# A three-stage layer on one core: the prologue and first pass in another order, six half-tile normalisings on the activation engine, and the last routing in one run

## The chip, the cores and the metric

The kernel runs on one core of one Trainium2 chip. TensorE (PE) multiplies matrices, VectorE (DVE) and ScalarE (ACT) work on elements, GpSimd (POOL) issues gathers and scatters with indices, SyncE (SP) issues the plain loads and stores. The metric is the device time in microseconds (us) of one launch; lower is better. The kernel before takes 1042.08 us (median of 3 runs, 1041.61 to 1042.24).

## The reference

```python
scores = scale * q @ k.T              # 4 x 8 heads, 576 positions, 64 wide
scores = where(0 <= i - j < 64, scores, -1e9)
x = softmax(scores) @ v               # window attention -> x: 2304 x 512
g = sigmoid(x @ w_gate) * (x @ w_val) # 512 -> 1536
x = g @ w_out                         # 1536 -> 512
noisy = x @ w_gate2 + log1p(exp(x @ w_noise)) * noise   # 8 experts
top2, weights = the two largest of noisy, softmax over the two
out[t] = sum over its two experts of weight * (relu(x[t] @ w1[e]) @ w2[e])   # 512 -> 1024 -> 512
```

Everything is float32. The dense layer's three weights are handed over as the 64-bit integers of doubles, which the kernel turns into float32 itself.

## The kernel before

Every large product is three matmuls, on a high and a low half of each operand (`mm3`, L55 to L58), so each operand must first be split: the high half by ACT, the low half by DVE.

The tokens stand in 18 tiles of 128 and 6 blocks of 3 tiles. The dense layer goes block by block; inside a block it goes over 12 slices `f` of 128 hidden columns. For a slice PE makes the gate and the value (12 matmuls of 384 columns each), ACT takes the tanh, DVE multiplies, ACT and DVE split the product, and PE adds it to the output (9 matmuls of 512 columns). The first block has more to do: its three tiles of attention must be there first, and during it the weights of each slice are converted, by three ACT steps (L187, L192, L222) and four DVE steps (L197, L202, L208, L231) on 128 x 1536 elements. Slice 0 is converted in thirds of 512.

The order of this prologue and first pass is written out by hand as a string of words, `FIRST`; each engine runs its part of it in that order. A letter is a step and a number the slice or attention tile; `a` and `b` are halves of four heads. The steps that the text speaks of:

- weights: `m` (ACT, L187), `r` (ACT, L192), `s` (DVE, L197), `o` (DVE, L202), `a` (DVE, L208), `h` (ACT, L216 or L222), `l` (DVE, L229 or L231). `r` and `a` share one buffer, `rnd`.
- attention of a tile: `S` scores (PE, L244), `M` mask and maximum (DVE, L258), `E` exponential (ACT, L269), `N` the sums' reciprocals (DVE, L274, L275) and the normalising of four heads (DVE, L280), `P` transposes (PE, L286), `C` their copy (ACT, L292), `O` times v (PE, L307), `H` and `X` the split of the result (ACT L316, DVE L321).
- the slice: `g` and `V` gate and value (PE), `t` tanh (ACT, L337), `u` multiply (DVE, L342), `q` and `w` the split (ACT L349, DVE L353), `y` output (PE, label acc).

`g0` and `V0` are cut: columns 0 to 255 (`a`) need tiles 0 and 1, the rest (`b`) needs tile 2, that is the third L321. All loads go out on SP's queue; before, they hang on certain words (`S0`, `O0`, `O2`) and on a list ahead of the string.

After the dense layer's last block come the last block's routing (`route_L1`, `La`, `Lb`, `Lc`, `P`, `Q`, on DVE with two small matmuls in `P`), the scatter of its rows into the experts' slot tables (POOL, L522), and the gather of the fifth tile of expert 0. PE meanwhile works on the first four tiles of expert 0: per slice `h_mm` (12 matmuls of 512 columns), `h_ev` (relu on ACT, low half on DVE, L711 and L712) and `y_mm`; `split_e` makes the halves of the next slice's weights (L654 to L657). Then the experts follow one after the other, eight slices each. At the end of an expert `y_out` scales the five tiles and scatters each by an adding DMA (POOL, L745).

Of the kernel before, what the change touches and what calls it, by code (L numbers as in the profile page):

```python
# [11 lines left out]
F32R = mybir.dt.float32r  # L12
# [3 lines left out]
AF = mybir.ActivationFunctionType  # L16
# [3 lines left out]
P = 128  # L20
# [15 lines left out]
CAP = CT * P  # L36
# [9 lines left out]
def build(nc, tc, a, out):  # L46
# [27 lines left out]
    qk0 = pa.tile([P, 4, P + 192], F32, name="qk", bufs=1)  # L74
# [46 lines left out]
    noise = const.tile([P, TT, 8], F32)  # L121
# [5 lines left out]
    with c1:  # L127
# [106 lines left out]
        Sp, Pt, PT, Ox = {}, {}, {}, {}  # L234
# [29 lines left out]
        def attn_E(t, cs):  # L264
            sm, st = Pt[t]
            for c in cs:
                if c not in En.setdefault(t, set()):
                    En[t].add(c)
                    nc.scalar.activation(sm[:, c], sm[:, c], AF.Exp, bias=st[:, 0, c:c + 1], scale=-1.0,  # L269
                                         accum_out=st[:, 1, c:c + 1])  # L270

        def attn_R(t, cs=slice(0, 8)):
            st = Pt[t][1]
            nc.vector.tensor_scalar(st[:, 1, cs], st[:, 1, cs], 1e-9, None, op0=OP.add)  # L274
            nc.vector.reciprocal(st[:, 2, cs], st[:, 1, cs])  # L275

        def attn_N(t, g):
            sm, st = Pt[t]
            c = slice(g * 4, g * 4 + 4)
            nc.vector.tensor_tensor(sm[:, c], sm[:, c], st[:, 2, c, None].to_broadcast([P, 4, P]), op=OP.mult)  # L280
# [97 lines left out]
        R = {}  # L378
# [152 lines left out]
        def fill_slots():  # L531
# [10 lines left out]

        FIRST = """
            r00 m00 s00 S0 o00 a00 h00 S1 M0b l00 E0b M0a M1b E0a M1a N0b r01 m02 N0a P0b m01 r02 s02 P0a o02
            E1a a02 S2 s01 o01 h02 a01 C0a E1b N1a M2b h01 N1b E2b l01 l02 C0b N2b m1 P1b M2a O0 r1 s1 o1 E2a
            S3 a1 C1b H0 P2b m2 X0 N2a P1a h1 s2 o2 C1a r2 O1 l1 C2b a2 m3 M3b H1 h2 X1 s3 P2a r3 l2 g0a
            C2a E3b o3 O2 m4 a3 V0a H2 s4 h3 X2 o4 g0b r4 V0b l3 t0 g1 u0 m5 a4 V1 q0 s5 r5 w0 M3a y0 t1 h4 u1
            o5 E3a g2 l4 q1 V2 w1 m6 N3a a5 t2 y1 s6 r6 g3 o6 h5 u2 S4 a6 q2 V3 w2 h6 l5 y2 t3 r7 l6 g4 m7 u3  # L550
            N3b q3 P3a s7 m8 V4 w3 o7 C3a t4 P3b u4 y3 C3b M4a q4 w4 E4a a7 y4 s8 h7 O3 o8 r8 g5 l7 H3 V5 t5
            X3 m9 a8 g6 u5 h8 s9 M4b V6 q5 r9 w5 l8 t6 y5 E4b u6 N4a q6 V7 N4b m10 w6 o9 g7 a9 P4a t7 y6 C4a u7
            h9 s10 o10 q7 g8 r10 l9 V8 a10 m11 P4b S5 w7 C4b s11 r11 y7 o11 h10 M5a O4 t8 M5b E5a g9 u8 l10 H4
            V9 q8 E5b w8 X4 N5a y8 t9 u9 a11 q9 S6 w9 P5a h11 N5b y9 C5a l11 P5b g10 C5b M6a O5 t10 V10 H5 X5
            g11 u10 q10 w10 V11 t11 y10 u11 q11 w11
        """
        SB = (("S0", "S1"), ("gate", "val"), ("acc0", "acc1"))

        def first(word):
            k, n = word[0], word[1:]  # L560
            if k in "mrsoahl":
                fn = {"m": cv_m, "r": cv_r, "s": cv_s, "o": cv_o, "a": cv_a, "h": cv_h, "l": cv_l}[k]
                if len(n) == 2 and n[0] == "0":
                    fn(0, slice(int(n[1]), int(n[1]) + 1))
                else:
                    fn(int(n))
                return
            if k in "gV":
                cols = {"a": slice(0, 2 * P), "b": slice(2 * P, BW)}.get(n[-1], slice(0, BW))
                glu_in(0, int(n.rstrip("ab")), "gV".index(k), cols)  # L570
                return
            g = "ab".find(n[-1])
            t = int(n.rstrip("ab"))
            heads = range(4 * g, 4 * g + 4)
            if k == "S":
                attn_S(t, SB[t] if t < len(SB) else ("S0", "S1"))
                if t == 0:
                    load_qk(3)
                    load_raw(2)
                elif t > 2:  # L580
                    load_qk(t + 1)
            elif k == "M":
                attn_M(t, heads)
            elif k == "E":
                attn_E(t, heads)
            elif k == "N":
                attn_R(t, slice(4 * g, 4 * g + 4))
                attn_N(t, g)
            elif k == "P":
                attn_PT(t, g, ("OP", "acc2")[g] if t < 3 else "OP")  # L590
            elif k == "C":
                attn_PC(t, g)
            elif k == "O":
                attn_O(t)
                if t == 0:
                    load_vv(3)
                    for f in range(3, 8):
                        load_raw(f)
                elif t > 2:
                    load_vv(t + 1)  # L600
                elif t == 2:
                    nc.sync.dma_start(noise, a["moe2_noise"].rearrange("(t p) e -> p t e", p=P))
                    fill_slots()
                    for f in range(8, NF1):
                        load_raw(f)
            elif k == "H":
                attn_XH(t)
            elif k == "X":
                attn_X(t)
            elif k == "y":  # L610
                glu_out(0, t)
            else:
                {"t": lambda f: glu_tanh(), "u": glu_mul, "q": glu_high, "w": glu_low}[k](t)

        nc.sync.dma_start(qk0[:, 0:1], a["qk"][0, :, 0:1])
        load_raw(0, (0,))
        nc.sync.dma_start(qk0[:, 1:4], a["qk"][0, :, 1:4])
        load_qk(1)
        load_vv(0)
        load_raw(0, (1, 2))  # L620
        load_vv(1)
        load_qk(2)
        load_vv(2)
        load_raw(1)
        for word in FIRST.split():
            first(word)


        NCH = NF2 // 2
        YB = ("gate", "val", "acc0", "acc1", "acc2")  # L630
        ep, rawc, sp = {}, {}, {}
# [73 lines left out]
                hp[e, f].append(o)  # L705

        def h_ev(e, f, cols=ALL):
            hh = ep[0].tile([P, CAP], F32R, tag="hh", name="hh", bufs=2)
            hl = ep[0].tile([P, CAP], F32R, tag="hl", name="hl", bufs=2)
            for o, c in zip(hp.pop((e, f)), cols):  # L710
                nc.scalar.activation(hh[:, c], o, AF.Relu)  # L711
                nc.vector.scalar_tensor_tensor(hl[:, c], o, 0.0, hh[:, c].bitcast(F32),  # L712
                                               op0=OP.max, op1=OP.subtract)
            hS[e, f] = (hh, hl)
# [134 lines left out]
        b = NB - 1  # L849
        pre = range(EARLY // P)  # L850
# [14 lines left out]
        route_L1(b)  # L865
        h_mm(0, 1, PRE)
        route_La(b)
        h_ev(0, 1, PRE)
        y_mm(0, 0, pre)
        split_e(2)  # L870
        h_mm(0, 2, PRE)
        route_Lb(b)
        h_ev(0, 2, PRE)
        route_Lc(b)
        y_mm(0, 1, pre)
        split_e(3)
# [34 lines left out]
    for n in range(NA, NE * NF2):  # L911
        e, f = divmod(n, NF2)
        h_mm(e, f)
        h_ev(e, f)
        split_e(n + 2)
        if n < NE * NF2 - 1:
            y_mm(*y_prev)
        if f == 0:
            for j in range(CT):
                y_out(e - 1, j)  # L920
        if 0 < e < NE - 1 and f >= NF2 - CT:
            xg_T(e + 1, f - NF2 + CT)
        if f == 0 and 0 < e < NE - 1:
            table(e + 1, slice(0, CT))
            gather(e + 1, slice(0, CT))
        y_prev = (e, f)
    for j in range(CT):
        for i in range(len(y_parts(NE - 1, j))):
            for f in (NF2 - 2, NF2 - 1):
                y_mm(NE - 1, f, (j,), (i,))  # L930
        y_out(NE - 1, j)
    ce.close()
# [82 lines left out]
```

## Time and profile before

| what | value |
|---|---|
| median of 3 runs | 1042.08 us |
| the profiled execution: time, span | 1041.44 us, 1039.6 us |
| PE busy | 1002.0 us (96%) |
| DVE, ACT, POOL busy | 577.6, 385.5, 153.2 us |
| granted clock of PE over the span | 0.981 |
| moved by DMA | 126.78 MB, mean 122 GB/s |

The profiled execution's time is 1.9 us over its span: the program's start and end lie around it. PE's busy share says little by itself, since its matmuls overlap; the idle time before a group, the chain that ended last and the start times in the timeline tell where it waits.

### The profile page before, as it was taken

How to read it: one execution, taken by the hardware profiler on the slowest of the kernel's cores; microseconds unless marked ns; L12 is line 12 of the kernel's file. 1: busy time of each engine (PE TensorE's matmuls, PEld its weight loads, DVE VectorE, ACT ScalarE, POOL GpSimd, SP SyncE). 2: the span in 40 equal slices, each digit the busy share in tenths (PEclk: the TensorE clock that was granted, in tenths of full speed). 3: DMA queues.
4: the chain of work that ended last, by engine and by line, in shares of the span. 5: the costliest groups of instructions: out<-in, count | busy, mean ns of one | idle time of the engine just before them, and what ended most of it. 6: DMA issues, size and time to landing. Idle time of an engine off the chain costs nothing.

```text
span 1039.6 us, 16682 instructions
## 1 busy us (share of the span) xinstructions
PE 1002.0 (96%) x6460; PEld 914.2 (88%) x6460; DVE 577.6 (56%) x1608; ACT 385.5 (37%) x874; POOL 153.2 (15%) x210
## 2 busy tenths in 40 slices
PE   4699999999999999999999999999999999999995
PEld 3699899999999999999998799999989999999994
DVE  7999657667767767774326434344334343434431
ACT  7887533233333333321114233333333333333321
POOL 0000000002000200302030505050311305050303
PEclk7799999999999999999999999999999999999998
DMA  8970322233333223336224417262443627172503
GB/s 344 351 280 21 133 88 83 94 117 93 102 117 107 93 101 118 83 103 219 76 70 164 128 58 192 71 161 103 93 133 92 171 82 182 44 181 82 92 1 54
DMA packets 56568, 126.78 MB, mean 122 GB/s; under 512 B 13968, under 2 KB 14112, under 8 KB 56480
## 3 DMA queue, kind: packets, MB, share of 16 engines
q1 hardware_dynamic: 46304, 104.56, 29.5%
q0 software_dynamic: 10176, 21.07, 10.0%
q8 instruction: 53, 0.87, 0.3%
q14 instruction: 35, 0.29, 0.1%
HBM read 101.11 MB, written 24.49 MB: 121 GB/s over the span
## 4 chain that ended last, share of the span: by engine, by line
PE 87%; issue 4%; DMA 3%; ACT 2%; POOL 1%; DVE 1%; SPq 0%; POOLq 0%; DVEq 0%; ACTq 0%
PE gv L56 10%; PE gv L57 10%; PE gv L58 10%; PE hp L58 6%; PE hp L57 6%; PE hp L56 6%; PE yacc L56 6%; PE yacc L57 6%; PE yacc L58 6%; PE acc L56 5%; PE acc L58 5%; PE acc L57 5%; DMA raw<-in_moe_w 2%; PE Op L307 2%; PE xgp L687 2%
## 5 line engine op out<-in xcount | busy, mean ns | idle before, releaser
L56 PE MATMUL gv<-xT,W 128*128 128x384 f32 (+2 forms) x584 | 201.2, 344 | 0.0
L57 PE MATMUL gv<-xT,W 128*128 128x384 f32 (+2 forms) x584 | 196.6, 337 | 0.8 <-DVE xT L321 0.8
L58 PE MATMUL gv<-xT,W 128*128 128x384 f32 (+2 forms) x584 | 196.6, 337 | 0.0
L712 DVE SCALAR_TENSOR_TENSOR hl<-hp,hh 128x320 fp32r<-128x320 f32 (+2 forms) x128 | 62.9, 491 | 199.8 <-ACT hh L711 197.7
L56 PE MATMUL hp<-xgT,h 128*128 128x320 f32 (+2 forms) x512 | 162.3, 317 | 0.0
L58 PE MATMUL hp<-xgT,l 128*128 128x320 f32 (+2 forms) x512 | 159.5, 312 | 0.0
L57 PE MATMUL hp<-xgT,h 128*128 128x320 f32 (+2 forms) x512 | 159.4, 311 | 0.0
L711 ACT ACTIVATE hh<-hp 128x320 fp32r<-128x320 f32 (+2 forms) x128 | 56.0, 438 | 219.7 <-PE hp L58 219.7
L420 DVE CUSTOM_DVE_ANT_0 dump<-x,wb 128x512 bf16<-128x512 f32 x192 | 132.1, 688 | 3.1
L56 PE MATMUL yacc<-h,hh 128*128 128x512 f32 (+1 forms) x328 | 127.5, 389 | 0.0
L57 PE MATMUL yacc<-l,hh 128*128 128x512 f32 (+1 forms) x328 | 127.1, 387 | 0.0
L58 PE MATMUL yacc<-h,hl 128*128 128x512 f32 (+1 forms) x328 | 126.8, 386 | 0.0
L522 POOL DMA_INDIRECT slots<-rec,sli x36 | 39.0, 1084 | 524.3 <-DMA wb<-in_wgn 249.4
L745 POOL DMA_INDIRECT out<-yo,tb x40 | 66.3, 1659 | 328.2 <-ACT yo L741 319.7
L56 PEld LDWEIGHTS gv<-xT,W 128*128 128x128 f32 x584 | 110.3, 189 | 4.1 <-issue 2.1
L57 PEld LDWEIGHTS gv<-xT,W 128*128 128x128 f32 x584 | 110.4, 189 | 2.6 <-DVE xT L321 0.9
L58 PEld LDWEIGHTS gv<-xT,W 128*128 128x128 f32 x584 | 110.3, 189 | 0.0
L342 DVE SCALAR_TENSOR_TENSOR th<-th,gv 128x384 f32<-128x384 f32 x72 | 39.8, 553 | 119.8 <-PE gv L58 100.1
L56 PEld LDWEIGHTS hp<-xgT,h 128*128 128x128 f32 x512 | 96.4, 188 | 2.2 <-DVE hl L712 0.4
L57 PEld LDWEIGHTS hp<-xgT,h 128*128 128x128 f32 x512 | 96.4, 188 | 1.9
L58 PEld LDWEIGHTS hp<-xgT,l 128*128 128x128 f32 x512 | 96.2, 188 | 1.3 <-DVE l L655 0.2
L56 PE MATMUL acc<-W,gH 128*128 128x512 f32 x216 | 86.4, 400 | 0.0
(137 smaller groups left out, 1526.2 us busy)
## 6 DMA issues: line engine op xcount, KB each, us to landing
raw<-in_moe_w SPq DMA_DIRECT2D x36, 512.0 KB
wb<-in_wgn SPq DMA_DIRECT2D x32, 512.0 KB
r<-in_w SPq DMA_DIRECT2D x32, 512.0 KB
r<-in_moe_w SPq DMA_DIRECT2D x32, 512.0 KB
qk<-in_qk SPq DMA_DIRECT2D x15, 640.0 KB
v<-in_v SPq DMA_DIRECT2D x32, 256.0 KB
out<-zero SPq DMA_DIRECT2D x26, 256.0 KB
xd<-x SPq DMA_DIRECT2D x6, 768.0 KB
```

The costliest lines, as they stand in the source:

```text
L56: nc.tensor.matmul(o, lh, rh, start=start, stop=False)
L57: nc.tensor.matmul(o, lh, rl, start=False, stop=False)
L58: nc.tensor.matmul(o, ll, rh, start=False, stop=stop)
L307: nc.tensor.matmul(o[h * 64:(h + 1) * 64, r * P + i * 64:r * P + (i + 1) * 64], v[:, i, r * P + h * 64:r * P + (h + 1) * 64], pt[:, c:c + 64],
L342: nc.vector.scalar_tensor_tensor(g, g, 1.0, gv.pop(1)[:, :BW], op0=OP.add, op1=OP.mult)
L420: nc.vector.tensor_tensor_reduce(out=dump, in0=x2[b][:, j], in1=WB[8 * b + c // 2][:, c % 2], op0=OP.mult, op1=OP.add, scale=1.0, scalar=0 ...
L522: st = nc.gpsimd.indirect_dma_start(out=slots, out_offset=bass.IndirectOffsetOnAxis(ap=sli[:, k, j:j + 1], axis=0), in_=rec[:, j, k, :], i ...
L687: nc.tensor.transpose(p[:, c], xg[:, c], ident)
L711: nc.scalar.activation(hh[:, c], o, AF.Relu)
L712: nc.vector.scalar_tensor_tensor(hl[:, c], o, 0.0, hh[:, c].bitcast(F32), op0=OP.max, op1=OP.subtract)
L745: st = nc.gpsimd.indirect_dma_start(out=out, out_offset=bass.IndirectOffsetOnAxis(ap=tb[:, j, 0:1].bitcast(I32), axis=0), in_=yo, in_offse ...
```

## The change

- `FIRST` is another string. Loads are words of it now (`K`: `Kr` raw weights, `Kq`, `Kz` q and k, `Kv` v, `Kf` the filler of the slot tables), so their order on SP's queue stands in the string; the noise comes last.
- `N` no longer takes the reciprocals along; they are the word `R`. `n` normalises four heads on ACT, one instruction for each; `n3b n3a n4a n4b n5b n5a` replace six `N`.
- `hh` and `hl` have three buffers instead of two.
- In the last routing `Lb`, `Lc` follow `La`, and `P`, `Q` follow the next `h_mm`, ahead of the `h_ev` that stood before them.
- The last expert's sixth slice is no longer added to the output between the last two `h_mm`, but with the last two slices, tile by tile.

```diff
         FIRST = """
-            r00 m00 s00 S0 o00 a00 h00 S1 M0b l00 E0b M0a M1b E0a M1a N0b r01 m02 N0a P0b m01 r02 s02 P0a o02
...
+            Kr00 Kq0 Kz0 Kr01 Kq1 Kv0 Kr02 m00 r00 Kv1 s00 o00 Kq2 a00 S0 Kv2 h00 m01 l00 Kr1 r01 Kf0 M0a Kq3
...
+            elif k == "R":
+                attn_R(t, slice(4 * g, 4 * g + 4))
             elif k == "N":
-                attn_R(t, slice(4 * g, 4 * g + 4))
                 attn_N(t, g)
+            elif k == "n":
+                sm, st = Pt[t]
+                for c in heads:
+                    nc.scalar.activation(sm[:, c], sm[:, c], AF.Copy, scale=st[:, 2, c:c + 1])
...
-        nc.sync.dma_start(qk0[:, 0:1], a["qk"][0, :, 0:1])
-        load_raw(0, (0,))
...
         for word in FIRST.split():
             first(word)
+        load_qk(7)
+        load_vv(6)
+        nc.sync.dma_start(noise, a["moe2_noise"].rearrange("(t p) e -> p t e", p=P))
...
-            hh = ep[0].tile([P, CAP], F32R, tag="hh", name="hh", bufs=2)
-            hl = ep[0].tile([P, CAP], F32R, tag="hl", name="hl", bufs=2)
+            hh = ep[0].tile([P, CAP], F32R, tag="hh", name="hh", bufs=3)
+            hl = ep[0].tile([P, CAP], F32R, tag="hl", name="hl", bufs=3)
...
         route_La(b)
+        route_Lb(b)
+        y_mm(0, 0, pre)
+        route_Lc(b)
         h_ev(0, 1, PRE)
-        y_mm(0, 0, pre)
         split_e(2)
         h_mm(0, 2, PRE)
-        route_Lb(b)
+        route_P(b)
+        route_Q(b)
         h_ev(0, 2, PRE)
-        route_Lc(b)
         y_mm(0, 1, pre)
         split_e(3)
-        route_P(b)
         h_mm(0, 3, PRE)
-        route_Q(b)
...
-        if n < NE * NF2 - 1:
+        if n < NE * NF2 - 2:
             y_mm(*y_prev)
...
-            for f in (NF2 - 2, NF2 - 1):
+            for f in range(NF2 - 3, NF2):
                 y_mm(NE - 1, f, (j,), (i,))
```

DVE in the prologue, before: from the second tile's `X` (L321) to the third's. `m0` and `m1` hold the even and odd slices in turn; `raw_332` is slice 3, `raw_336` slice 4.

```order
L321 TENSOR_TENSOR xT_312<-Op_404,xT_312 128x4x128
L197 TENSOR_SCALAR m1_122<-m1_122 128x1536
L231 TENSOR_TENSOR W_433<-m0_121,W_433 128x3x512
L202 SCALAR_TENSOR_TENSOR m1_122<-raw_332,m1_122 128x1536
L536 TENSOR_SCALAR early_120<-early_120 128x144
L537 TENSOR_SCALAR early_120<-early_120 128x144
L208 ISA m1_122<-m1_122,rnd_125 128x3072
L197 TENSOR_SCALAR m0_121<-m0_121 128x1536
L321 TENSOR_TENSOR xT_312<-Op_464,xT_312 128x4x128
```

DVE at the same place, changed: from the third tile's `X` on (`raw_337` is slice 3).

```order
L321 TENSOR_TENSOR xT_288<-Op_459,xT_288 128x4x128
L208 ISA m0_121<-m0_121,rnd_125 128x3072
L197 TENSOR_SCALAR m1_122<-m1_122 128x1536
L202 SCALAR_TENSOR_TENSOR m1_122<-raw_337,m1_122 128x1536
L342 SCALAR_TENSOR_TENSOR th_542<-th_542,gv_437 128x384
L231 TENSOR_TENSOR W_419<-m1_122,W_419 128x3x512
```

The last step of slice 2 (L208) and all steps of slice 3 stand behind the third `X` now; before, slice 3 and the first step of slice 4 stood ahead of it.

ACT in the last routing, before, from the routing's first exponential (`u`) on; `hh` is the relu of a slice, `h` the high halves of the next slice's weights, `ee` the routing's second exponential.

```order
L435 ACTIVATE u<-u 128x24
L711 ACTIVATE hh<-hp 128x512
L654 ACTIVATE h_5705<-r_5574 128x512
L656 ACTIVATE h_5707<-r_5575 128x512
L465 ACTIVATE ee<-ee 128x6
```

ACT at the same place, changed.

```order
L435 ACTIVATE u<-u 128x24
L465 ACTIVATE ee<-ee 128x6
L712 ACTIVATE hh<-hp 128x512
L655 ACTIVATE h_5745<-r_5592 128x512
L657 ACTIVATE h_5747<-r_5593 128x512
```

`ee`, which waits for DVE's `Lb`, moved ahead of the relu of slice 1 and of the weights of slice 2.

## Rows read from the trace of the kernel before

**Rows 1.** Windows: busy us (and count) of PE, PEld, DVE, ACT, POOL, clock, DMA.
```profile
46.00:54.00 8.00, 7.35 (x49) 7.28 (x50) 8.00 (x14) 6.51 (x7) 0.00 (x0) 1.00 0.94 299
```

**Rows 2.** Chain that ended last, prologue and first pass: start us, us, what.
```profile
5.02 1.28 ACT L192
6.31 0.67 ACT rnd L192
...
45.99 0.61 DVE xT L321
...
71.79 0.44 PE PTp L286 x4
...
78.95 1.08 PE Op L307 x32
```

**Rows 3.** Timeline of PE, end of the first pass: start us, us, what.
```profile
128.46 0.40 PE L57 MATMUL acc<-W,gH 128*128 128x512 f32 x1
...
128.93 0.34 PE L56 MATMUL gv<-xT,W 128*128 128x384 f32 x1
129.11 0.34 PE L57 MATMUL gv<-xT,W 128*128 128x384 f32 x1
```

**Rows 4.** DVE's groups up to 126 us: busy us, mean ns, idle before us.
```profile
L202 DVE SCALAR_TENSOR_TENSOR m<-raw,m 128x1536 int32<-128x1536 int32 x11 | 19.3, 1755 | 0.2
L208 DVE CUSTOM_DVE_ANT_0 m<-m,rnd 128x3072 uint16<-128x3072 uint16 x11 | 19.3, 1752 | 0.2
L231 DVE TENSOR_TENSOR W<-m,W 128x1536 fp32r<-128x1536 f32 x11 | 19.2, 1752 | 0.1
L197 DVE TENSOR_SCALAR m<-m 128x1536 int32<-128x1536 int32 x11 | 10.5, 953 | 0.0
L258 DVE CUSTOM_DVE_ANT_0 sm<-Sp,mask 128x128 f32<-128x128 f32 x36 | 8.2, 286 | 0.6 <-PE PTp L286 0.6
L353 DVE TENSOR_TENSOR gL<-th,gH 128x384 fp32r<-128x384 f32 x11 | 6.1, 553 | 0.6 <-ACT gH L349 0.6
...
L280 DVE TENSOR_TENSOR sm<-sm,st 128x512 f32<-128x512 f32 x8 | 5.5, 692 | 0.3
```

**Rows 5.** Timeline of ACT, the exponential of one head.
```profile
10.46 0.39 ACT L269 ACTIVATE sm<-sm,st 128x128 f32<-128x128 f32 x1
```

**Rows 6.** Windows, columns as in rows 1: a stretch at half clock.
```profile
30.30:43.90 13.60, 8.22 (x80) 7.41 (x82) 13.46 (x22) 11.75 (x18) 0.00 (x0) 0.50 1.02 408
```

**Rows 7.** Timeline of DVE in the last routing.
```profile
565.20 0.18 DVE L448 SCALAR_TENSOR_TENSOR q<-q,s 128x24 f32<-128x24 f32 x1
...
567.10 0.18 DVE L455 SCALAR_TENSOR_TENSOR q<-lg,q 128x24 f32<-128x24 f32 x1
...
572.60 0.57 DVE L491 TENSOR_TENSOR base<-posp,base 128x8 f32<-128x8 f32 x3
...
574.70 0.16 DVE L512 TENSOR_TENSOR rec<-ee,smr 128x6 f32<-128x6 f32 x1
```

**Rows 8.** Timeline of ACT in the last routing.
```profile
564.18 0.62 ACT L654 ACTIVATE h<-r 128x512 fp32r<-128x512 f32 x1
...
568.56 0.21 ACT L465 ACTIVATE ee<-ee 128x6 f32<-128x6 f32 x1 [3.23 <-DVE ee L464]
```

**Rows 9.** Timeline of PE in the last routing and at the late gather.
```profile
566.21 0.39 PE L56 MATMUL hp<-xgT,h 128*128 128x512 f32 x1
...
593.81 1.09 PE L687 MATMUL xgp<-ident,xg 128*128 128x128 f32 x4 [2.59 <-DMA xg<-xd,tb]
```

**Rows 10.** Windows, columns as in rows 1: behind the late gather.
```profile
593.50:596.90 3.40, 3.09 (x10) 2.63 (x11) 1.33 (x3) 1.63 (x3) 2.48 (x4) 0.50 0.70 207
```

**Rows 11.** Timeline at the end of the program.
```profile
1023.28 1.55 POOL L745 DMA_INDIRECT out<-yo,tb  x1 [39.33 <-ACT yo L741]
...
1027.84 0.48 DVE L743 TENSOR_SCALAR yo<-yacc,tb 128x256 f32<-128x256 f32 x1 [0.68 <-issue]
...
1030.73 1.56 POOL L745 DMA_INDIRECT out<-yo,tb  x1 [0.27 <-issue]
```

More of the change, by code (lines that the diff above doesn't have):

```diff
@@ L545, in build @@
         FIRST = """
-            r00 m00 s00 S0 o00 a00 h00 S1 M0b l00 E0b M0a M1b E0a M1a N0b r01 m02 N0a P0b m01 r02 s02 P0a o02
[L547 to L555, printed above, removed]
+            Kr00 Kq0 Kz0 Kr01 Kq1 Kv0 Kr02 m00 r00 Kv1 s00 o00 Kq2 a00 S0 Kv2 h00 m01 l00 Kr1 r01 Kf0 M0a Kq3
+            M0b E0a S1 Kr2 s01 o01 E0b a01 R0a M1a h01 N0a E1a R0b P0a N0b M1b P0b r02 C0a R1a S2 N1a m02 C0b
+            l01 E1b s02 o02 O0 M2b R1b E2b M2a a02 Kv3 H0 N1b h02 X0 P1b m1 R2b Kr3 N2b P1a l02 C1b S3 s1 C1a r1
+            o1 O1 Kq4 E2a a1 Kr4 P2b H1 Kr5 R2a m2 N2a X1 Kr6 h1 M3b P2a s2 Kr7 V0a C2b l1 C2a E3b O2 o2 r2 g0a
+            R3b H2 M3a m3 X2 Kr8 a2 g0b E3a Kr9 V0b s3 Kr10 t0 h2 o3 g1 Kr11 r3 u0 l2 V1 q0 n3b w0 a3 t1 y0 m4
+            u1 R3a h3 V2 s4 o4 q1 n3a S4 w1 r4 P3a l3 y1 Kq5 C3a a4 m5 P3b g2 M4a C3b r5 s5 O3 o5 t2 E4a g3 u2
+            Kv4 a5 q2 h4 V3 w2 h5 R4a l4 y2 t3 r6 u3 l5 g4 q3 H3 m6 w3 X3 y3 M4b m7 s6 o6 E4b V4 s7 t4 n4a g5 u4
+            R4b q4 a6 n4b V5 w4 h6 o7 y4 t5 r7 u5 l6 S5 q5 w5 P4a m8 a7 y5 Kq6 C4a s8 h7 P4b o8 g6 r8 M5b C4b V6
+            a8 t6 E5b M5a O4 h8 u6 S6 R5b l7 q6 Kv5 r9 w6 g7 m9 l8 n5b s9 y6 o9 t7 m10 V7 a9 E5a s10 g8 h9 u7
+            R5a q7 o10 V8 n5a r10 w7 l9 y7 t8 H4 u8 m11 X4 V9 a10 q8 w8 P5a h10 s11 g9 o11 C5a r11 y8 l10 t9 u9
+            P5b a11 g10 q9 C5b M6a h11 O5 w9 V10 t10 l11 H5 X5 g11 u10 q10 w10 V11 t11 u11 y9 y10 q11 w11
         """
@@ L560, in first @@
             k, n = word[0], word[1:]
+            if k == "K":
+                k, n = n[0], n[1:]
+                if k == "r":
+                    if n[0] == "0":
+                        load_raw(0, (int(n[1]),))
+                    else:
+                        load_raw(int(n))
+                elif k == "f":
+                    fill_slots()
+                elif k == "v":
+                    load_vv(int(n))
+                elif n == "0":
+                    rs = slice(0, 1) if k == "q" else slice(1, 4)
+                    nc.sync.dma_start(qk0[:, rs], a["qk"][0, :, rs])
+                else:
+                    load_qk(int(n))
+                return
             if k in "mrsoahl":
@@ L576, in first @@
                 attn_S(t, SB[t] if t < len(SB) else ("S0", "S1"))
[L577 to L581, printed above, removed]
             elif k == "M":
@@ L594, in first @@
                 attn_O(t)
[L595 to L605, printed above, removed]
             elif k == "H":
@@ L613, in first @@
                 {"t": lambda f: glu_tanh(), "u": glu_mul, "q": glu_high, "w": glu_low}[k](t)
-        nc.sync.dma_start(qk0[:, 0:1], a["qk"][0, :, 0:1])
-        load_raw(0, (0,))
[L617 to L624, printed above, removed]
         for word in FIRST.split():
             first(word)
+        load_qk(7)
+        load_vv(6)
+        nc.sync.dma_start(noise, a["moe2_noise"].rearrange("(t p) e -> p t e", p=P))
         NCH = NF2 // 2
```

## The prediction

> **What bounds the kernel now.** I read the page first: PE is busy for 96% of the span, which its overlapping matmuls make look fuller than it is. So I read the idle column of the groups and the start times in PE's timeline. From the third L321 on, at 46.65 us, PE's matmuls follow each other at the same spacing (0.175 us for 384 columns, 0.235 for 512 [rows 3]) nearly everywhere up to the last expert's end. Three places are left: the 46.65 us ahead of that, a wait of 2.59 us for a late gather up to 593.81 [rows 9], and the scatters behind the last matmul. The change has an edit for each.
>
> The windows show who sets the first place: in 46 to 54 us DVE is busy for 8.00 of 8 us and ACT for 6.51 [rows 1]. The chain of waits begins with the table load at 5.02, goes on over ACT and DVE, and ends with the third `X` at 45.99 [rows 2]. The chain names two raw loads ahead of it, but DVE worked through them without a gap, so I take DVE's list and not the loads as the bound. From 46.65 PE runs 82.3 us to the end of `y10` at 128.93 [rows 3].
>
> **A. Prologue and first pass.** First the way to the third `X`. Ahead of it stand, fewer than before, two L208, two L197, one L202 and one L231: 3.50 + 1.91 + 1.76 + 1.75 = 8.92 us [rows 4]. New ahead of it are four L258 of tile 3 (4 x 0.29 = 1.14) and a pair for the reciprocals, some 0.4. Net 7.4 us less.
>
> The start moves too. The raw weights are now the first load instead of the second, and `m00` stands before `r00`, so that `s00` doesn't wait for an `r` of 0.67 [rows 2]; together some 1.0 us earlier. Behind `a00` no maximum stands any more, so that `l00` waits for ACT's `h00`, some 0.7 us. Net 0.3 us. The third `X` then ends near 38.9 instead of 46.6: PE could run 7.75 us earlier.
>
> It can't keep all of that. Between the third `X` and `l7`, DVE's list in the new order has 7 L208, 6 L202, 6 L231, 6 L197, 13 short ones of the slices (L342 is as long as L353), 16 L258, four reciprocal pairs and one L321. By rows 4, with the 0.07 us by which a next instruction starts before the row's duration is over, that is 49.4 us. PE's list from there to `g7` has 12 gates or values (12 x 12 x 0.175 = 25.2), six outputs (6 x 9 x 0.235 = 12.7), the two cut ends (2.7), and nine pieces of attention: four transposes of 0.44, three S and two O, an S being as long as the O of 1.08 [rows 2], 7.1 in all. That is 47.7. So PE comes to `g7` about 1.7 us before DVE has made its weights; this is the new tightest place, near 88.5. Behind it PE has ten gates or values, five outputs and two us of attention, 33.5 by the same count. The count gives 81.1 for the whole stretch that took 82.3, so I add 1.5%: 34.0. The end of `y10` comes at 122.5, 6.4 us earlier than 128.93.
>
> Of the six normalisings, four lie before `l7`; each takes 0.69 us off DVE [rows 4], 4.15 in all. On ACT one becomes four instructions. The nearest row is a head's exponential, 0.39 [rows 5], 1.2 us for four when they overlap, 1.6 when not: 7 to 9.4 us more on ACT. Before `l7` it is 4.8 in 49.4 us, or 0.8 per 8 us, which takes ACT from 6.5 to 7.3 of 8. The idle rest hides it, but thinly; waits between the engines will grow. Before L353 alone DVE waited 0.6 us in the whole pass [rows 4]; I allow as much again. **A = -5.8 us.** Bounds: -7.7 if PE never waits, and -4.1 if DVE stays full to its last step, so that only its own 3.8 (the six, overlapped) and the 0.3 count.
>
> On that move the Trainium skill speaks against the change: "ScalarE: Activation LUTs", Rules for kernel authors, gives multiplications to VectorE rather than ScalarE. The rows agree that the step is dearer on ACT, 1.2 to 1.6 us against 0.69. By the rule the six cost 7 to 9.4 us and spare 4.15; that matters only where ACT is the one that is late, which is the first rival.
>
> I cost the loads at nothing. They were all on SP's queue before. Slice 1's raw weights stand in both orders behind the same small loads; the filler is written earlier and the noise goes last, where the router's weights behind it have another slice's time before their first use. If that cover is missing, the second block's first router products come late, on an engine that has slack by then.
>
> **B. The last routing.** DVE's `Lb` starts when `La` ends, at 565.4, instead of 567.10 [rows 7], so ACT's `ee` comes 1.7 us earlier, at 566.86 instead of 568.56 [rows 8]. But now the relu of slice 1 and the weights of slice 2 are queued behind `ee` on ACT: the weights' high half, at 564.18 before [rows 8], is there near 568.1 after 0.2 for `ee` and two steps of about 0.6. PE wants it at 566.21 [rows 9]. So PE gets a new wait of 1.9 us, and 0.45 more for the low half that DVE makes behind it. The two small matmuls of `P` then run near 571.5, since `h_mm` ahead of them is late too. DVE's part from L491 to the records took from 572.60 to 574.86 [rows 7]; it now runs 0.9 us earlier, and so does the chain of scatter, table and gather up to 593.81 [rows 9]. DVE then makes slice 3's low half behind `Q`: another 0.5 for PE. PE comes to the gather 2.9 us later, near 594.0, and finds it done. The wait has moved, not gone: +0.15 us. What can be won is the stretch behind it, 3.4 us at clock 0.50 [rows 10], where PE, idle for its first 0.3, lost half of the rest, 1.5. Whether a split hole of 1.9, 0.45 and 0.5 us costs the clock as well, no row shows. Bounds: -1.5 with the clock kept, +1.7 with a second such stretch. I take -0.6, nearer to the first. **B = -0.6 us.**
>
> **C. The end.** POOL's five scatters start at 1023.28 and then 1.86 us apart, to 1030.73 [rows 11], though PE makes a tile every 1.4 us: POOL is the bound. In the new order the sixth slice's matmuls stand inside the tiles, so that a tile takes nine matmuls, 2.05 us, instead of six. PE's work and its end stay, but the tiles begin earlier: the first one is done four times 0.7 us, or 2.8, sooner. The first scatter then starts near 1020.4 and POOL keeps up. The last tile's last half is ready as before, its DVE step running 1027.84 to 1028.32 [rows 11], so that the last scatter starts near 1028.6, 2.1 us earlier. If the scatters themselves queue behind each other, the whole row comes 2.9 us earlier, as the first does. Third buffers of `hh` and `hl` make the order possible and cost nothing else. **C = -2.6 us**, between -2.1 and -2.9; these ends are narrow because all of it lies behind known work.
>
> **Sum.** -5.8 - 0.6 - 2.6 = -9.0 us. The profiled execution took 1041.44; it would take 1032.4. The median of the runs is 0.64 over that execution: **1033.1 us**.
>
> **The rivals.**
>
> *ACT paces the first pass.* For it: ACT's 1.5 idle us per 8 [rows 1] are waits for DVE and PE, which need not shrink when its work grows. If they stay, 0.8 more per 8 us makes the 49.4 us before `l7` 4.8 us longer. Against it: `h`, `m` and `r` stand ahead of need in the new string. A = -1.0, in all -4.2: 1037.9.
>
> *PE's clock stays down once more.* PE ran at half clock from 30.3 to 43.9 [rows 6], 13.6 us, with its work in short pieces; in the new string PE begins in pieces again, near 32, with two cut halves before the third `X`. One such stretch on dense work loses 6.8 us, of which 1.7 is the wait for `l7`: A = -0.7, in all -3.9, 1038.2. The Trainium skill, "TensorE: Matmul & The Clock Gate", Part 1, says the same in its words: the throttled state is the default and activity releases it. Against it: before, the clock was full from 43.9 on, where PE's pieces had just begun to follow each other.
>
> *The same, twice: slower.* If PE's small waits behind each `w` and `l` keep it at half clock from 38.9 for two stretches, to 66, it loses 13.6 - 1.7 = 11.9 us, and A becomes +6.1; with B and C +2.9: 1045.0. It decides from some 22 us of half clock on. Against it: PE's waits after 39 should be under 1 us each up to `g7`.
>
> *The string brings nothing.* Raw loads and not DVE could set 45.99, as the chain has it; then A is about 0, and B and C give 1038.9. Against it stands the DVE row that is full.
>
> **How the numbers follow.** Forecast 0.72; ACT paces 0.10; one clock stretch 0.06; nothing from the string 0.07; two stretches or an unnamed loss of that size 0.05. The likeliest case alone spans the bounds of A, B and C: 1042.1 - 12.1 = 1030.0 to 1042.1 - 4.5 = 1037.6. With the next cases the range is 1029.8 to 1038.6. 0.2%, about what a measurement of this kernel can tell from no change, is 2.1 us: all cases but the last are faster by more, and some of the worst corners are not. Faster 0.91, same 0.04, slower 0.05.
>
> **What would show it.** A: the third L321 near 39 instead of 46, `y10` ending near 122.5, PE idle before the gates of slice 7 for a DVE L231. ACT's waits before L222 and L349 tell its rival; a clock under 1.00 after 45 us tells the other. B: PE idle for an ACT L655 near 561 (566 less A) and none at the gather. C: five POOL scatters 2.0 us apart. I am wrong if `y10` ends later than 125, or if the gather still holds PE.

## The result, and the profile after

The changed kernel takes 1031.17 us (median of 6 runs, 1029.98 to 1034.24) against 1041.91 (6 runs, 1041.59 to 1042.88): ratio 0.9905 (95% interval 0.989 to 0.992), 10.7 us less. Forecast were 1033.1, in a range of 1029.8 to 1038.6. The profiled execution is one of the two longest of the six, 1034.13 us with a span of 1032.3, so it shows only 7.3 us of the gain; what the other runs have more is found below.

The prologue first. ACT's timeline (start us, us, what, idle before and what ended it) answers to the table load of [rows 2]:

```profile
0.76 1.28 ACT L187 ACT_TABLE_LOAD   x1 [0.76 <-PEq L1006]
4.48 0.66 ACT L187 ACTIVATE m<-raw 128x512 f32<-128x512 f32 x1 [2.44 <-DMA raw<-in_moe_w]
5.04 0.67 ACT L192 ACTIVATE rnd<-raw 128x512 int32<-128x512 uint32 x1
```

DVE's first step on the weights and the third `X`, which answers to 45.99 of [rows 2]:

```profile
5.17 0.43 DVE L197 TENSOR_SCALAR m<-m 128x512 int32<-128x512 int32 x1 [1.25 <-ACT m L187]
...
36.55 0.69 DVE L321 TENSOR_TENSOR xT<-Op,xT 128x512 fp32r<-128x512 f32 x1
```

PE at the foreseen tight place, and at the end of the first pass, which answers to [rows 3]:

```profile
87.25 0.34 PE L57 MATMUL gv<-xT,W 128*128 128x384 f32 x1
87.74 0.44 PE L58 MATMUL gv<-xT,W 128*128 128x384 f32 x1 [0.15 <-DVE W L231]
...
121.17 0.39 PE L58 MATMUL acc<-W,gL 128*128 128x512 f32 x1
121.40 0.33 PE L56 MATMUL gv<-xT,W 128*128 128x384 f32 x1
```

The third `X` starts 9.4 us earlier; `y10`, whose last matmul is the one at 121.17, ends 7.5 us earlier. The table load no longer stands behind the wait for the raw weights but in it. And PE hardly waits before the gates of slice 7.

Then the last routing. On ACT (to be read with [rows 8]) the relu and the weights do queue behind `ee`:

```profile
559.30 0.21 ACT L465 ACTIVATE ee<-ee 128x6 f32<-128x6 f32 x1 [4.44 <-DVE ee L464]
559.42 0.58 ACT L712 ACTIVATE hh<-hp 128x512 fp32r<-128x512 f32 x1
559.90 0.62 ACT L655 ACTIVATE h<-r 128x512 fp32r<-128x512 f32 x1
```

PE's three waits there, the last at the gather, answer to [rows 9]:

```profile
560.57 0.50 PE L56 MATMUL hp<-xgT,h 128*128 128x512 f32 x1 [1.78 <-ACT h L655]
...
569.19 0.50 PE L58 MATMUL hp<-xgT,l 128*128 128x512 f32 x1 [0.26 <-DVE l L656]
...
589.06 0.63 PE L688 MATMUL xgp<-ident,xg 128*128 128x128 f32 x4 [0.97 <-DMA xg<-xd,tb]
```

The first wait is the one foreseen, 1.78 us for ACT's L655. The gather is still waited for, though less than the 2.59 of before. And the stretch at half clock (0.50, which is 1.2 of 2.4 GHz) now lies between the two; the first line is another one, in the first pass, which the second profile of this kernel does not have (windows; columns as in [rows 1]):

```profile
39.86:43.28 3.42, 3.42 (x13) 3.42 (x13) 3.42 (x3) 3.42 (x6) 0.00 (x0) 0.50 1.03 412
...
562.10:565.50 3.40, 3.40 (x12) 2.66 (x10) 0.00 (x0) 0.06 (x1) 0.00 (x0) 0.50 0.00 0
```

At the end, POOL's five scatters answer to [rows 11]. Four of them wait for the tile that ACT or DVE scales out of PE's result, not for the scatter ahead; for the last one's 0.59 us the profile names no engine:

```profile
1014.28 1.55 POOL L746 DMA_INDIRECT out<-yo,tb  x1 [36.54 <-ACT yo L742]
...
1016.39 1.56 POOL L746 DMA_INDIRECT out<-yo,tb  x1 [0.51 <-DVE yo L744]
...
1018.36 1.56 POOL L746 DMA_INDIRECT out<-yo,tb  x1 [0.38 <-ACT yo L742]
...
1020.65 1.56 POOL L746 DMA_INDIRECT out<-yo,tb  x1 [0.69 <-DVE yo L744]
...
1022.84 1.56 POOL L746 DMA_INDIRECT out<-yo,tb  x1 [0.59 <-issue]
```

### The profile page after: what moved, and what is told of

Read it like the earlier page. It is cut to its first block, busy times and chain, and to the rows that moved or that the text cites. A ratio compares the mean times of both kernels' runs of the same rounds, so it can differ in the third digit from the quotient of the medians.

```text
span 1032.3 us, 16703 instructions
## 1 busy us (share of the span) xinstructions
PE 1001.0 (97%) x6460; PEld 911.8 (88%) x6460; DVE 573.4 (56%) x1602; ACT 392.2 (38%) x898; POOL 152.9 (15%) x210
## 4 chain that ended last, share of the span: by engine, by line
PE 91%; DVE 5%; issue 1%; DMA 1%; ACT 1%; POOL 0%; POOLq 0%; DVEq 0%; ACTq 0%
PE gv L56 10%; PE gv L58 10%; PE gv L57 10%; PE hp L58 7%; PE hp L57 7%; PE hp L56 7%; PE yacc L56 7%; PE yacc L57 7%; PE yacc L58 7%; PE acc L56 5%; PE acc L58 5%; PE acc L57 5%; PE xgp L688 2%; PE Op L307 1%; PE Sp L244 1%; PE PTp L286 1%
```

## The experiments

My theory after this reading: the first part brings 7.5 us and more, the routing costs 1.3, the end brings 1.0 to 1.6. The rival is the prediction's own sizes: 5.8, 0.6 and 2.6 less. All times below are medians; each ratio (its 95% interval in brackets) is to runs of the kernel before on the same chip, since between chips one kernel differed by 1.6 us. For each profile I also read three stages: (1) up to the first matmul of the dense layer's last output, (2) from there to the end of the last matmul, (3) from there to the end of the span.

| kernel | median, us | ratio to before | profiled: 1 | 2 | 3 |
|---|---|---|---|---|---|
| before | 1041.91 | 1 | 550.41 | 477.39 | 11.76 |
| changed | 1031.17 | 0.9905 [0.989, 0.992] | 542.85 | 478.70 | 10.79 |
| changed, again | 1030.77 | 0.9904 [0.9884, 0.9923] | 541.63 | 476.88 | 10.50 |
| order alone | 1033.58 | 0.9917 [0.9903, 0.993] | 543.00 | 476.29 | 12.50 |
| routing alone | 1041.25 | 0.9993 [0.9983, 1.0003] | 550.83 | 476.01 | 11.88 |
| end alone | 1041.06 | 0.9982 [0.9973, 0.9991] | 551.11 | 478.87 | 10.48 |
| old routing | 1033.30 | 0.9912 [0.9896, 0.9927] | 544.76 | 477.61 | 9.67 |
| `r` ahead of `m` | 1032.54 | 0.9912 [0.9899, 0.9925] | 543.50 | 476.67 | 10.33 |
| `N` on DVE | 1033.29 | 0.9916 [0.9903, 0.9929] | 544.68 | 477.05 | 9.90 |
| both of these | 1035.54 | 0.9935 [0.9922, 0.9949] | 548.30 | 476.90 | 9.83 |
| load later | 1030.53 | 0.9889 [0.9871, 0.9906] | 541.46 | 476.79 | 10.20 |
| mended routing | 1026.82 | 0.9864 [0.9846, 0.9881] | 541.73 | 473.39 | 9.99 |
| mended, again | 1028.39 | 0.9874 [0.9854, 0.9894] | 542.13 | 474.67 | 10.09 |
| mended, on before | 1038.79 | 0.9962 [0.9948, 0.9975] | 553.49 | 474.62 | 12.22 |

**The parts one by one.** Each of the first three leaves one part in; the fourth takes the routing out of the changed kernel. The order alone:

```diff
-            hh = ep[0].tile([P, CAP], F32R, tag="hh", name="hh", bufs=3)
+            hh = ep[0].tile([P, CAP], F32R, tag="hh", name="hh", bufs=2)
...
         route_La(b)
-        route_Lb(b)
+        h_ev(0, 1, PRE)
         y_mm(0, 0, pre)
-        route_Lc(b)
-        h_ev(0, 1, PRE)
...
-            for f in range(NF2 - 3, NF2):
+            for f in (NF2 - 2, NF2 - 1):
```

> The change's first part alone: the new string of the prologue and first pass with its loads and the six normalisings on ACT; the last routing and the end as before. Theory (the profile after, read by parts): it brings 7.5 us, 1.3 of them because ACT loads its table during its first DMA wait: end of y10 near 121.4, table load near 0.8, about 1034.4 us, 7.5 below the kernel before, and more than two thirds of the whole change. Rival 1 (the prediction's size): 5.8 us, 1036.1, y10 near 122.5. Rival 2 (a gain at y10 that is lost later in the same first half): y10 near 121.4 but less than 5 us at the end.

Measured: 8.4 us less, more than either size; `y10` ended at 121.55. The theory's place holds and the prediction's 5.8 doesn't. In stage 2 the wait for the gather was there, 3.0 us, with no half clock behind it.

The routing alone, and the end alone, put their lines of the change into the kernel before (with the third buffers):

```diff
         route_La(b)
+        route_Lb(b)
+        y_mm(0, 0, pre)
+        route_Lc(b)
         h_ev(0, 1, PRE)
...
```

> The new order of the last routing alone, with three buffers of hh and hl, on the kernel before. Theory: the order costs 1.3 us, since the wait ahead of slice 1's gate and the stretch at half clock move into the routing and the gather is still waited for: about 1043.2 us, PE waiting some 1.8 us for an ACT L655 near 566 and some 1 us for the gather. Rival (the prediction): 0.6 us less, 1041.3, no wait at the gather. A third possibility is that the cost differs from run to run, with a half-clock stretch in some and not in others: then the times are spread over some 3 us, or in two groups.

```diff
-        if n < NE * NF2 - 1:
+        if n < NE * NF2 - 2:
...
-            for f in (NF2 - 2, NF2 - 1):
+            for f in range(NF2 - 3, NF2):
```

> The new order of the end alone (the sixth slice's matmuls inside the tiles), with three buffers of hh and hl, on the kernel before. Theory (the profile after): first scatter 2.75 us earlier against PE's end, the last one 1.6 us earlier, since each scatter waits for the one before it on POOL: 1.0 to 1.6 us less, about 1040.6. Rival (the prediction): POOL keeps up, 2.6 us less, 1039.3.

The routing alone gave 0.7 us less, with an interval that reaches from 1.8 less to 0.3 more, so it is not told apart from no change. Its runs were spread over 3.1 us, but so were those of the kernel before beside it (4.4), and the third possibility stays open. Its profile, of the third fastest of eleven runs, is the prediction's step B nearly word for word: PE waits where it was to wait, and comes to the gather when the gather is done (PE's timeline):

```profile
568.52 0.50 PE L56 MATMUL hp<-xgT,h 128*128 128x512 f32 x1 [1.71 <-ACT h L654]
...
575.58 0.50 PE L58 MATMUL hp<-xgT,l 128*128 128x512 f32 x1 [0.24 <-DVE l L655]
...
594.32 0.60 PE L687 MATMUL xgp<-ident,xg 128*128 128x128 f32 x4
```

So the theory's +1.3, read from one run, is not borne out. The end alone gave 0.9 by the medians and 1.9 by the ratio. Its scatters stood as the theory had them, against PE's end 2.75 us earlier for the first and 1.65 for the last; that POOL keeps up is out. Its profile had two stretches at half clock in stage 2, at 562.4 and 596.5, the first with no wait of PE near it.

> The changed kernel with the last routing in the order of before; all else as changed. Theory 1 (the routing order costs 1.3 us): about 1.3 us below the changed kernel when both are profiled, 1032.8 against the profiled 1034.1, with PE's wait for the gather back at some 2.6 us and no wait for ACT L655 near 560. Theory 2 (the routing order saves 0.6 us or, in most of its runs, some 3 us): 0.6 to 3 us over the changed kernel's median, 1031.8 to 1034, and its runs lie close together, while the changed kernel's had two groups. It is to be compared with the sum of the first and the third of these kernels' differences: if the parts add up, the two agree within 0.5 us.

```diff
         route_La(b)
-        route_Lb(b)
-        y_mm(0, 0, pre)
-        route_Lc(b)
         h_ev(0, 1, PRE)
+        y_mm(0, 0, pre)
...
```

Measured 1033.30, 2.1 over the changed kernel's median on another chip, 0.7 by the ratios; its runs lay within 1.5 us. Theory 1 falls: by either figure this order is not the faster one. The sign speaks for theory 2, but 0.7 lies inside the intervals. By ratio the order and the end alone add up to 10.5 us; this kernel had 9.2. The two differ by more than the 0.5 us named ahead, though not by more than the intervals.

**The changed kernel again.**

> The changed kernel as it is, profiled a second time, beside the three others. Its six runs stood at 1034.2 (two, the profiled one among them) and 1030.0 to 1031.4 (four). Theory: the routing is what differs, by a half-clock stretch of 3.41 us there (1.5 to 1.7 us of loss, and the small matmuls of P that much later) and by the time from the first record's scatter to the first gather (17.2 us in the profiled run, 15.1 before): a profile of about 1031 shows no half clock near 560 and no wait at the gather over 0.3 us, and the same times up to y10 and behind PE's last matmul. Rival: the difference lies in the prologue (loads that land later) or behind the last matmul (the last scatter's landing, 5.6 us).

Again two of six runs stood apart, at 1034.0 and 1035.6. The profiled run was one of the other group, 1030.85, 3.3 us below the first. The clock fell here too, but elsewhere (windows):

```profile
33.80:46.00 12.20, 11.74 (x102) 10.91 (x102) 12.13 (x21) 11.98 (x23) 0.00 (x0) 1.00 1.03 408
...
552.62:556.04 3.42, 3.42 (x9) 2.63 (x8) 2.72 (x17) 0.22 (x1) 0.00 (x0) 0.50 1.04 389
```

Of the 3.3 us, 1.2 lie in stage 1: the full clock from 33.8 on, where the first profile lost the stretch from 39.86. 1.8 lie in stage 2. The half clock came ahead of the late `h` instead of behind it, so PE was slow while it would have waited: its step into `h_mm` then took 0.3 us more than usual instead of 1.9. The theory had the routing right but for the gather, and the first pass wrong; the rival named the prologue, but for its loads. The wait at the gather is there in this run as well, 0.72 us. That I had not expected of a run of this length.

**Why the start was worth more.** The first two words swapped back:

```diff
-            Kr00 Kq0 Kz0 Kr01 Kq1 Kv0 Kr02 m00 r00 Kv1 s00 o00
+            Kr00 Kq0 Kz0 Kr01 Kq1 Kv0 Kr02 r00 m00 Kv1 s00 o00
```

> The changed kernel with the first two words of its string swapped back: r00 ahead of m00 on the first raw weights. Theory: ACT's table load follows the wait for those weights again, since L192 waits for two engines and the load's wait stands by itself ahead of the table load: table load near 2.5 to 5 instead of 0.76, the first L197 1.3 to 1.9 us later than 5.17, and because DVE is the bound the third L321 and y10 as much later: 1.3 to 1.9 us over the changed kernel. Rival (the order of two short steps is hidden, as the rest of the prologue waits for other loads): first L197 later by 0.7 us or less, y10 unchanged within 0.3 us, same time.

ACT's timeline, then DVE's:

```profile
4.41 1.28 ACT L192 ACT_TABLE_LOAD   x1 [4.41 <-DMA raw<-in_moe_w]
5.70 0.66 ACT L192 ACTIVATE rnd<-raw 128x512 int32<-128x512 uint32 x1
6.27 0.66 ACT L187 ACTIVATE m<-raw 128x512 f32<-128x512 f32 x1
```

```profile
6.96 0.43 DVE L197 TENSOR_SCALAR m<-m 128x512 int32<-128x512 int32 x1 [3.03 <-ACT m L187]
...
38.30 0.68 DVE L321 TENSOR_TENSOR xT<-Op,xT 128x512 fp32r<-128x512 f32 x1
```

L197 came 1.8 us later than in the changed kernel, the third `X` 1.7, `y10` 1.8 (121.94 against 120.17 in the second profile) and the median 1.8. The last matmul of `y10`, in the second profile of the changed kernel and here:

```profile
119.94 0.39 PE L58 MATMUL acc<-W,gL 128*128 128x512 f32 x1
```

```profile
121.71 0.39 PE L58 MATMUL acc<-W,gL 128*128 128x512 f32 x1
```

The theory stands to the tenth: nothing between the first load and `y10` absorbs a late start. Where L192 comes first, the trace has the wait for the load as an instruction of its own, and the table load behind it (4.41 us idle, ended by the DMA); where L187 comes first, the table load goes ahead of the wait, and its line has no such instruction before 21.6 us (from the views of the two lines, here and in the changed kernel: ns shortest, median and longest, then first and last start):

```profile
L192 ACTq EVENT_SEMAPHORE  x3: 17/38/38, 4.4 to 86.2; - x3
```

```profile
L187 ACTq EVENT_SEMAPHORE  x16: 17/38/1591, 21.6 to 98.3; - x16
```

L187 waits for the load alone. L192 waits for DVE as well, which at the start still reads the buffer that `rnd` takes over. That this second wait makes the difference is my reading; the runs show only that the order of the two does. The Trainium skill, "ScalarE: Activation LUTs", What ACT_TABLE_LOAD costs, gives 1283 ns for the table load; the rows agree, 1.28. What it costs the kernel hung on what stood ahead of it.

**Who bounds the first pass.** The six normalisings back on DVE:

```diff
-            R3b H2 M3a m3 X2 Kr8 a2 g0b E3a Kr9 V0b s3 Kr10 t0 h2 o3 g1 Kr11 r3 u0 l2 V1 q0 n3b w0 a3 t1 y0 m4
+            R3b H2 M3a m3 X2 Kr8 a2 g0b E3a Kr9 V0b s3 Kr10 t0 h2 o3 g1 Kr11 r3 u0 l2 V1 q0 N3b w0 a3 t1 y0 m4
...
```

> The changed kernel with the six half-tile normalisings back on DVE, at the same places of the string. Theory (DVE bounds the first pass): DVE has 4 x 0.69 = 2.8 us more ahead of l7, and PE, which waits there for 0.3 us now, waits 2.5 to 3 us; y10 2.5 to 3 us later, about 1034. Rival 1 (PE's own work bounds the pass, and ACT has become as full as DVE): y10 within 0.5 us, the same time. Rival 2 (ACT paced by the moved work): y10 earlier, a faster kernel.

`y10` ended at 123.23, 3.1 us later than in the second profile, and the median was 2.5 higher: with the six on DVE, DVE is the bound, and "ACT paces" is out. One expectation was wrong. The loss doesn't stand in one wait before slice 7; it is spread, and this list has 1.8 us of the 3.1 (PE's waits from 45 to 125 us: for what, us in total, times, longest):

```profile
PE gv L58 <- DVE W L231: 0.8, 1, 0.8
PE gv L56 <- DVE th L342: 0.6, 3, 0.2
PE acc L58 <- DVE gL L353: 0.4, 2, 0.2
```

In the second profile of the changed kernel that list has one row, L231, with 0.2: there PE's own work is level with DVE's. ACT's room is used up as well. From 37.2 to 86.3 us it was busy for 40.6 of 49.1 us with the six on DVE, and for 47.5 with the six on ACT. The Trainium skill, "ScalarE: Activation LUTs", Rules for kernel authors, would put a multiplication on VectorE. Here the dearer engine was the right one by 2.5 us, because it was the one with time to spare.

Both reverted, so that only the words' order and the loads are left:

```diff
-            Kr00 Kq0 Kz0 Kr01 Kq1 Kv0 Kr02 m00 r00 Kv1 s00 o00
+            Kr00 Kq0 Kz0 Kr01 Kq1 Kv0 Kr02 r00 m00 Kv1 s00 o00
...
-            R3b H2 M3a m3 X2 Kr8 a2 g0b E3a Kr9 V0b s3 Kr10 t0 h2 o3 g1 Kr11 r3 u0 l2 V1 q0 n3b w0 a3 t1 y0 m4
+            R3b H2 M3a m3 X2 Kr8 a2 g0b E3a Kr9 V0b s3 Kr10 t0 h2 o3 g1 Kr11 r3 u0 l2 V1 q0 N3b w0 a3 t1 y0 m4
...
```

> The changed kernel with both: r00 ahead of m00 and the six normalisings on DVE. What is left of the first part is the order of the other words and the loads. Theory (the two gains are separate and DVE bounds the pass): 1.8 and 2.5 us, found one by one, add up: about 1035.1, first L197 near 7, y10 near 124.8. Rival (both give the same slack of DVE, found twice): 2.5 to 3 us in all, about 1033.5.

1035.54, on another chip: 4.8 over the changed kernel's second median, or 3.2 to 4.2 if the chip's own difference (0.6 for the kernel before, 1.6 for the mended one) is taken off; 3.2 by the ratios too. That lies between the rival's 3 and the sum of 4.3, and decides nothing. Nor does the profile: the third `X` came 1.8 us later, as the theory has it, and `y10` ended at 126.85 instead of 124.8, but this run was the longest of five and had 6.8 us of half clock from 40.7 on. The order and the loads without these two gave 6.8 us by the ratio with the routing and the end, whose ratios were worth 0.7 and 1.9; that leaves some 4 us. How much of it the loads' new places bring was not tried.

**The routing mended.** The prediction said that the wait was moved, not gone. If so, an order in which ACT makes the high halves of slices 2 and 3 ahead of `ee`, and DVE the low half of slice 3 between its routing steps, should lose both:

```diff
         route_La(b)
-        route_Lb(b)
-        y_mm(0, 0, pre)
-        route_Lc(b)
         h_ev(0, 1, PRE)
+        y_mm(0, 0, pre)
         split_e(2)
+        low1, low2 = split_e(3, True)
         h_mm(0, 2, PRE)
+        route_Lb(b)
+        route_Lc(b)
+        low1()
         route_P(b)
         route_Q(b)
         h_ev(0, 2, PRE)
+        low2()
         y_mm(0, 1, pre)
-        split_e(3)
         h_mm(0, 3, PRE)
```

(`split_e(3, True)` makes only the two high halves, and returns the low ones to be made later.)

> The changed kernel with the last routing mended: the relus and high halves that ACT makes for slices 1, 2 and 3 stand ahead of the routing's softmax again, so that PE has its operands when it comes, but DVE's part of the routing stays in one run, and DVE's low halves of slice 3 stand between its pieces. Theory (the moved wait costs 1.9 + 0.4 us, and the late records make the gather 1 us late in some runs): no wait of PE over 0.4 us between 550 and 590, the records on POOL about 2.5 us earlier against the last acc matmul than in the changed kernel, no wait at the gather: 2.3 to 3.5 us below the changed kernel, about 1028.3. Rival 1 (the waits are there in place of each other; PE's own count of columns sets the end): within 0.5 us of the changed kernel. Rival 2 (the half-clock stretch comes without a hole too): PE waits gone, the stretch still there, 0.5 to 1.7 us less than the theory's gain.

> The mended kernel a second time, for its times and a second profile. Expected: a median of 1026.5 to 1027.5, no wait of PE over 0.4 us between 550 and 590, none at the gather; if a stretch at half clock falls into the routing in this profile, it costs up to 1.7 us there, and the run is near 1028.5 or above; if none, near 1026.8.

> The kernel before with the mended routing alone, where the routing as changed gave about 0.7 us. Theory (the new wait of 1.9 + 0.4 us and the old one of 2.6 us at the gather are both gone, and nothing of it hangs on the new prologue): 3.5 to 5 us below the kernel before, about 1037.5; the end's order is untouched. Rival (the gain needs the new prologue or the new end): less than 2 us.

In both its profiles the list of PE's waits from 550 to 590 us is empty. POOL's timeline in the first shows the records and the gather early enough, and PE's first step on the gathered tile has no wait ahead of it. The margin is small: from the gather's start to the step that waited for it 3.6 us passed before and in the changed kernel (590.20 to 593.81, 585.46 to 589.06), and here there are 4.0:

```profile
563.79 1.00 POOL L522 DMA_INDIRECT slots<-rec,sli  x1 [30.31 <-DVE rec L512]
...
573.94 1.50 POOL L678 DMA_DIRECT2D tb<-slots  x2 [2.72 <-DMA slots<-rec,sli]
...
578.62 1.03 POOL L684 DMA_INDIRECT xg<-xd,tb  x1 [3.18 <-issue]
```

```profile
582.65 0.60 PE L697 MATMUL xgp<-ident,xg 128*128 128x128 f32 x4
```

1026.82 us, 3.95 under the changed kernel on the same chip and a little more than the theory's 3.5; on another chip 1028.39, over the 1026.5 to 1027.5 expected. By the ratios the two are 4.2 and 3.1 us better than the changed kernel. That is the best version of all: 0.9864 [0.9846, 0.9881] of before. Put into the kernel before it gave 4.0 us by the ratio, where the routing as changed gave 0.7, so the gain needs neither the new prologue nor the new end. In its second profile the half clock came in the routing with no wait of PE near it (windows), and stage 2 was 1.3 us longer:

```profile
549.00:552.88 3.88, 3.88 (x30) 3.64 (x29) 2.19 (x4) 1.63 (x3) 0.00 (x0) 1.00 1.02 404
552.88:556.29 3.41, 3.41 (x9) 2.67 (x8) 2.74 (x16) 0.22 (x1) 0.00 (x0) 0.50 1.03 390
```

So rival 2 holds for some runs. What PE did just before it fell are the router's 24 matmuls of 16 columns, from 549.63 to 552.36; the first profile has them too, and no fall.

**A load moved that didn't move.** In the changed kernel 17.2 us pass from the first record's scatter to the first gather (568.22 to 585.46), 17.1 in its second profile, 15.1 before. POOL's table read and gather, and SP's pair of weight loads:

```profile
580.05 1.49 POOL L669 DMA_DIRECT2D tb<-slots  x2 [4.16 <-DMA slots<-rec,sli]
585.46 1.03 POOL L675 DMA_INDIRECT xg<-xd,tb  x1 [3.92 <-issue]
```

```profile
579.20 0.34 SPq L640 DMA_DIRECT2D r<-in_w  x1
579.80 0.37 SPq L641 DMA_DIRECT2D r<-in_moe_w  x1
```

The pair, 1 MB, starts just ahead of the table's read. So I wrote it one slice later:

```diff
...
-            split_e(f)
+            split_e(f, f != 5)
+            if f == 6:
+                load_e(5)
```

> The changed kernel, with one pair of weight loads of the experts (1 MB in all, two of SP's) issued one slice later, behind the split of slice 6 instead of 5. In the changed kernel it starts at 579.20 in the profiled run and 576.36 in the second, within 1 us of POOL's reads of the table (580.05 and 577.35), and the first gather follows those by 5.4 and 5.1 us; in the kernel before the pair starts 4.8 us ahead of the table's read and the gather follows by 3.1 us. Theory (the table's read shares the DMA engines with that load): first gather about 3.3 us behind the table's read, 15.4 us behind the first record's scatter instead of 17.1, no wait of PE for the gather over 0.3 us, about 0.9 us less time, 1030. Rival (the read is slow for another reason, the scatters just ahead of it or the read's own length): 17 us from scatter to gather and 0.8 to 1.1 us of wait, as before; same time.

```profile
576.22 0.34 SPq L640 DMA_DIRECT2D r<-in_w  x1
```

The pair still started 1.1 us ahead of the table's read at 577.35, and the gather came 4.9 us behind that, with a wait of PE of 0.65: SP's queue had nothing ahead of the load and started it as soon as its buffer was free (DVE's L656, the step before it in the trace, ended at 576.2), wherever it was written. The run tells nothing about the cause, and its median of 1030.53 is the changed kernel's. What stands is the list of all fourteen profiles: in the eight with the pair at the read or up to 1.1 us ahead of it the gather follows by 4.5 to 5.4 us, in the six with the pair 4.6 to 4.8 us ahead of it or some 0.4 behind it by 3.0 to 3.7. That speaks for the shared DMA engines, but is not shown.

## Why the prediction came out as it did

By the medians of the table's profiles the three parts are: stage 1 from 550.97 (four with the old string) to 542.13 (seven with the new one), -8.8; stage 2 from 477.50 (old routing) to 476.88 (as changed), -0.6; stage 3 from 12.05 to 10.15, -1.9. The sum, -11.3, stands beside -10.7 and -11.4 in the times. Forecast were -5.8, -0.6 and -2.6. The time came out near the forecast because A was forecast too small and C too large, and this is partly luck: A's -8.8 lies outside its bounds of -7.7 and -4.1, and with C at its 2.6 the time would have been some 0.7 us less, near 1030.5, at the low end of the range.

**A, -5.8 forecast, -8.8 measured, outside its bounds.** The step that failed is "The start moves too", "Net 0.3 us". I gave the first load and `m00` ahead of `r00` 1.0 us and took 0.7 off. DVE's first L197 came 2.4 us earlier (7.56 to 5.17): 0.6 because the load landed earlier, and 1.8 by the swap, of which I had seen only `r`'s 0.67. The table load's 1.28, which stood in [rows 2], I took as fixed to the head of ACT's work. The rest of the count held. From the end of the third `X` to `l7` I had 49.4 us, and it took 49.1 in the second profile (50.4 in the first, with half clock in it); behind that 34.0, and it took 33.9 and 33.7. The 1.7 us of PE's wait before slice 7 were 0.3 by the step from 87.25 to 87.74: PE's own count of 47.7 was some 1.4 too low. DVE set the time, as said, but by so little that PE was almost the bound itself. So of the 3.0 us that A missed, 1.7 stand at the third `X`, 1.4 of these from the start; 0.6 are the further waits that I had allowed for and that didn't come; the last 0.7 are counts that were a little long. `l00` did wait 0.7 for `h00`. In stage 1 the stretches of half clock behind the third `X` made the rest of the spread: with the whole first part in place `y10` ended at 120.0 to 120.7 with none there, 121.4 and 121.55 with 3.4 us, 123.2 with 6.8 us.

**B, -0.6 forecast, -0.6 by the medians.** The agreement confirms little: the profiles of either order spread over more than 2.5 us in stage 2, and the routing alone was not told apart from no change. The new wait was foreseen at 1.9 us, 0.45 for slice 2's low half and 0.5 for slice 3's. Against the usual step of 0.23 the routing alone lost 1.9 at the first place, 0.2 at the second (0.47 from 568.86 to 569.33) and 0.4 at the third. DVE's L491 was to start 0.9 us ahead of 572.60; in the routing alone it ran at 572.07, in a profile that was 0.4 us later by then. The step that failed is that PE comes to the gather "and finds it done". It held in the routing alone; in all six profiles with this routing and the new start PE still waited, for 0.6 to 1.0 us, which the prediction had named as a sign of being wrong. From the scatter to the gather I took the 15.1 us of before, and it was 16.9 to 17.3; why, stays open. Whether the hole costs the clock I had left open. The runs say that the clock falls in or behind the routing in most profiles (eleven of fourteen), hole or not. Ahead of the hole, as in the second profile of the changed kernel, the slow stretch takes most of the wait's place; behind it, as in the first, it adds to the wait.

**C, -2.6 forecast, -1.9 measured.** The first scatter came 2.75 us earlier against PE's end, as forecast (2.8). The failing step is that the last one starts "2.1 us earlier": it starts 1.29 us behind PE's end instead of 2.93, 1.64 earlier, and 1.28 or 1.29 in all ten profiles with the new end. I had let it follow DVE's step by 0.28; it took 0.77, and the profile names no engine for the last 0.59. The rest of the stage, from the last scatter to the end of the span, was 8.4 to 9.6 us whichever the order, so that stage 3 tells no more than these 1.64.

The rivals: "ACT paces" and "the string brings nothing" fell by two experiments. One more stretch at half clock came in part: 3.4 us of it in some runs, at a loss of 1.2. Two of the size that makes it slower came in neither of the changed kernel's profiles.

## What to carry to other kernels

Before an engine's first table function, look what waits ahead of it: the same load is free inside a wait and costs its full length behind one. A wait that an order removes on one engine is looked for on the engine whose queue it lengthens; if PE's operands stand behind the long chain there, put them ahead of it and cut the other engine's work into the chain's gaps. And take a second profile before the place of a loss is believed: here two profiles of one kernel differed by a third of the gain.

## What the runs showed of the hardware

The granted clock fell to 0.50 in stretches of 3.4 us and longer, at places that differ from run to run of one kernel: in the routing at 562.1 in one profile of the changed kernel and at 552.6 in the next, at 552.9 in one of the mended kernel and nowhere in the other. What decides it stays open. One of 3.4 us on dense work cost 1.2 us in the first pass and 1.3 in the routing, each told from two profiles of one kernel; one of 6.8 us in the first pass cost 3.0, told from the old routing's `y10` (123.2) against the changed kernel's second (120.2).
